# Whole-width loads, a contiguous gMLP, and the V loads on ScalarE's queue in a decode step of attention plus gMLP

## The chip, the cores and the metric

The kernel runs on one core of a Trainium2 chip. The core has five engines with instruction streams of their own: TensorE (PE; its weight loads are listed as PEld), VectorE (DVE), ScalarE (ACT), GpSimd (POOL) and SyncE (SP). Loads and stores are done by 16 DMA engines, to which SP, ACT and POOL hand work through queues; each such engine issues its DMAs in the order of its own instruction stream. The metric is the device time of one execution in microseconds. A profiled execution gives a span (first to last instruction) and a trace.

## What is computed

x is a batch of 4 rows of 640 numbers, normalized to xn. One branch is attention of one query token over a cache of 4096 keys and values, for 32 heads of 128, the other a gMLP block with a hidden size of 864 after the split:

```python
    x = A_x
    xn = _layernorm(x, axis=-1)
    return x + _A_ref(xn, A_k_cache, A_v_cache, A_wq, A_wo) + _B_ref(xn, B_w_in, B_w_sp, B_b_sp, B_w_out)
```

```python
    q = (lambda x, *d: x.transpose(*d))((x @ wq).reshape(B, Sq, H, Dh), 0, 2, 1, 3)
    scores = jnp.einsum('bhqd,bhkd->bhqk', q, k_cache) * Dh ** (-0.5)
    p = _softmax(scores, axis=-1)
    o = jnp.einsum('bhqk,bhkd->bhqd', p, v_cache)
    return (lambda x, *d: x.transpose(*d))(o, 0, 2, 1, 3).reshape(B, Sq, H * Dh) @ wo
```

```python
    z = _gelu(jnp.einsum('bsd,df->bsf', x, w_in))
    z1 = z[..., :Fh].copy()
    z2 = _layernorm(z[..., Fh:], axis=-1)
    g = jnp.einsum('ts,bsf->btf', w_sp, z2) + b_sp[None, :, None]
    return jnp.einsum('bsf,fd->bsd', z1 * g, w_out)
```

The K and V caches are bfloat16 and hold 134 MB each; every byte of them is read once.

## The kernel before

The cache is cut into 32 units of K and 32 of V, called K0 to K31 and V0 to V31 here. A unit is four heads of one batch row, 4096 KB, laid over all 128 partitions, 32 KB in each. Four units in a row (the four batch rows) share their four heads and form one of 8 groups; a softmax is done once for each group.

All big loads share one pool of five buffers, `kvpool`, of one unit each (L66, L85): first the gMLP weights w_in and w_out (L98, L100; w_out on 108 partitions, since 864 = 8 x 108), then the query weights wq in two parts (L107), then K and V units in turn (`load_unit`, L283). A load into a buffer waits until the buffer's last user is done. All of these loads are issued by SP, which has hardly anything else in its stream and so stands waiting at the next free buffer. The output weights wo of a group come into a buffer of their own (`load_wo`, L291). For groups 5 and 6 that load is cut by partitions into 112, 8, 8 and 112, 12, 4 (L464); the last group's comes in three parts by head, ahead of V31 in SP's stream. V31 itself is loaded in four pieces (L475).

A static loop over steps (L476) writes the work down. In a step VectorE transposes a quarter of a K unit (`emit_T`, L305; two buffers for its result), TensorE multiplies the quarter before it with the queries (`emit_S`, L323), and a quarter of a V unit that lies 18 steps behind is multiplied with the probabilities (`emit_V`, L409). At the end of a group come the maximum (L330, L334, L345), the exponentials on ScalarE (L351), their transposes on TensorE (L364), and the copies on ScalarE which place them in `Zb` (L375). After each second V unit ScalarE copies the sums out of PSUM (`emit_O`, L417). The pool for those copies has three buffers and is shared with the probabilities p (tags at L350 and L416). Every four V units the output projection adds to `proj` (L447), an accumulator in PSUM that the kernel opened with x times an identity (L195).

The loop's order is not yet the order on the engines. The framework orders each engine's instructions by its own planner when the program is built, gives the pool's buffers out in that order, and adds the semaphores. What an engine waits for is then fixed: an instruction in an engine's stream stands behind all those before it.

V31 is handled apart: its 128 slices of 128x128 are weights of small matmuls (L520) that follow the pieces as they land; then come the last product with 1/rowsum (L521), the last projection, one copy (L525) and two stores (L526, L527).

At the start, x comes over ScalarE's queue (L92), the two scalars w_sp and b_sp of the gMLP over GpSimd's (L203, L204). VectorE copies the scalars (L215, L216), does the layer norm (L123 to L136), and TensorE does the gMLP's first product in 80 matmuls (L212), whose weights are read from w_in at a stride of 8 elements.

Of the kernel before, what the change touches and what calls it, by code (L numbers as in the profile page):

```python
# [8 lines left out]
ACT = mybir.ActivationFunctionType  # L9
ALU = mybir.AluOpType  # L10
AX = mybir.AxisListType
F32 = mybir.dt.float32
BF16 = mybir.dt.bfloat16
# [3 lines left out]
def kernel(  # L17
# [19 lines left out]
    nc = tc.nc  # L37
    P = 128
    B, Sq, D = A_x.shape
    _, H, Sk, Dh = A_k_cache.shape  # L40
    assert Sq == 1 and B == 4 and Dh == P and D % P == 0
    DC = D // P
    HG = 4
    M = P // HG
    T = Sk // M
    NCH = 4
# [3 lines left out]
    NG = H // HG  # L50
    NU = NG * B
    G = HG * B
    F2 = B_w_in.shape[1]
    Fh = F2 // 2
    FC = next(c for c in range(1, Fh + 1) if Fh % c == 0 and Fh // c <= P)
    FP = Fh // FC
    NOUT = A_wo.shape[1]
    NH = 2
    NO2 = NOUT // NH
    scale = float(Dh) ** -0.5  # L60
    eps = 1e-5
    VD = B * NCH + 2

    const = ctx.enter_context(tc.tile_pool(name="const", bufs=1))
# [4 lines left out]
    wopool = ctx.enter_context(tc.tile_pool(name="wopool", bufs=1))  # L69
# [4 lines left out]
    ps_g = ctx.enter_context(tc.tile_pool(name="ps_g", bufs=1, space=bass.MemoryType.PSUM))  # L74
# [4 lines left out]
    def misc_ps(shape, dtype):  # L79
        misc_ctr[0] += 1  # L80
        return ps_m.tile(shape, dtype, tag="misc", name=f"misc{misc_ctr[0]}")

    KV = T * Dh

    def kv_tile(name):  # L85
        return kvpool.tile([P, KV], BF16, tag="kv", name=name)


    x_flat = A_x.rearrange("b s d -> (b s) d")
    out_flat = out.rearrange("b s d -> (b s) d")  # L90
    x_bf = const.tile([B, D], BF16)
    nc.scalar.dma_start(out=x_bf[:], in_=x_flat)  # L92


    wg = kv_tile("w_gmlp")
    n_in = DC * F2
    w_in = wg[:, 0:n_in].rearrange("p (c f) -> p c f", c=DC)
    nc.sync.dma_start(out=w_in, in_=B_w_in.rearrange("(p c) f -> p c f", c=DC))  # L98
    w_out = wg[:FP, n_in:n_in + FC * NOUT].rearrange("p (c n) -> p c n", c=FC)
    nc.sync.dma_start(out=w_out, in_=B_w_out.rearrange("(p c) n -> p c n", c=FC))  # L100

    wq_v = A_wq.rearrange("(p c) n -> p c n", c=DC)
    wq_t = []
    for i, (c0, c1) in enumerate(((0, 3), (3, DC))):
        wt = kv_tile(f"wq{i}")
        n = (c1 - c0) * H * Dh
        nc.sync.dma_start(out=wt[:, 0:n].rearrange("p (c n) -> p c n", c=c1 - c0), in_=wq_v[:, c0:c1, :])  # L107
        for c in range(c0, c1):
            wq_t.append(wt[:, (c - c0) * H * Dh:(c - c0 + 1) * H * Dh])


    ident_bf = const.tile([P, P], BF16)
# [3 lines left out]
    ones_f = const.tile([P, P], F32)  # L116
    nc.vector.memset(ones_f[:], 1.0)
    eps_t = const.tile([P, 1], F32)
# [1 line left out]

    lnb = wt[:B, KV // 2:KV // 2 + 6 * D].bitcast(F32)
    xf, xc, sq = lnb[:, 0:D], lnb[:, D:2 * D], lnb[:, 2 * D:3 * D]
    nc.vector.tensor_copy(out=xf, in_=x_bf[:])  # L123
    ssum = small.tile([B, 1], F32, tag="ln_s")
    nc.vector.reduce_sum(out=ssum[:], in_=xf, axis=AX.X)
    negmean = small.tile([B, 1], F32, tag="ln_m")
# [38 lines left out]
    for bb in range(2):  # L165
        nc.vector.tensor_copy(out=SelG[:, bb, :, :, 2 * bb:2 * bb + 2],
                              in_=I32[:].rearrange("p (b h c) -> p c h b", b=2, c=NCH))
# [13 lines left out]
    for hd in range(HG):  # L181
        nc.vector.tensor_copy(out=Pm[:, :, hd, :].rearrange("p (a w) j -> p a w j", w=2),
                              in_=ident_bf[:].rearrange("p (a j w) -> p a w j", a=2, w=2))
# [7 lines left out]


    proj = ps_j.tile([64, 512], F32)
    for hf in range(NH):
        nc.tensor.matmul(proj[32 * hf:32 * hf + 32, 0:NO2], lhsT=ident_bf[:B, 0:32],  # L195
                         rhs=x_bf[:, hf * NO2:(hf + 1) * NO2], start=True, stop=False)


    wsp_bf = const.tile([P, 1], BF16)
    bsp_bf = const.tile([P, 1], BF16)  # L200
    wsp_f = const.tile([P, 1], F32)
    bsp_f = const.tile([P, 1], F32)
    nc.gpsimd.dma_start(out=wsp_bf[:], in_=B_w_sp.rearrange("a b -> (a b)").to_broadcast((P, 1)))  # L203
    nc.gpsimd.dma_start(out=bsp_bf[:], in_=B_b_sp.to_broadcast((P, 1)))  # L204

    zT_ps = ps_g.tile([FP, 2, FC, B], F32)

    for fc in range(FC):
        for part in range(2):
            w = w_in[:, :, part * Fh:(part + 1) * Fh].rearrange("p c (f a) -> p c a f", a=FC)  # L210
            for c in range(DC):
                nc.tensor.matmul(zT_ps[:, part, fc, :], lhsT=w[:, c, fc, :],  # L212
                                 rhs=xnT[:, c, :], start=(c == 0), stop=(c == DC - 1))

    nc.vector.tensor_copy(out=wsp_f[:], in_=wsp_bf[:])  # L215
    nc.vector.tensor_copy(out=bsp_f[:], in_=bsp_bf[:])  # L216
    zT = const.tile([FP, 2, FC, B], F32)
    nc.scalar.activation(out=zT[:], in_=zT_ps[:], func=ACT.Gelu_apprx_tanh)  # L218
    z1 = zT[:, 0, :, :]
    z2 = zT[:, 1, :, :]  # L220
    st_in = const.tile([FP, 2, FC, B], F32)
    nc.vector.tensor_copy(out=st_in[:, 0], in_=z2)  # L222
    nc.vector.tensor_tensor(out=st_in[:, 1], in0=z2, in1=z2, op=ALU.mult)
    st_ps = misc_ps([FP, 2, FC, B], F32)
    nc.tensor.matmul(st_ps[:].rearrange("p s c b -> p (s c b)"), lhsT=ones_f[:FP, :FP],
                     rhs=st_in[:].rearrange("p s c b -> p (s c b)"), start=True, stop=True)
    st = const.tile([FP, 2, B], F32)
    nc.vector.tensor_reduce(out=st[:], in_=st_ps[:].rearrange("p s c b -> p s b c"), axis=AX.X, op=ALU.add)
    mean = const.tile([FP, B], F32)
    nc.vector.tensor_scalar(out=mean[:], in0=st[:, 0, :], scalar1=1.0 / Fh, scalar2=None, op0=ALU.mult)  # L230
    msq = const.tile([FP, B], F32)
    nc.vector.tensor_tensor(out=msq[:], in0=mean[:], in1=mean[:], op=ALU.mult)
    var = const.tile([FP, B], F32)
    nc.vector.scalar_tensor_tensor(out=var[:], in0=st[:, 1, :], scalar=1.0 / Fh, in1=msq[:],
                                   op0=ALU.mult, op1=ALU.subtract)
    rs = const.tile([FP, B], F32)
    nc.scalar.activation(out=rs[:], in_=var[:], func=ACT.Sqrt, bias=eps_t[:FP, 0:1], scale=1.0)
    nc.vector.reciprocal(out=rs[:], in_=rs[:])
# [12 lines left out]
    for h in range(H):
        for c in range(DC):
            nc.tensor.matmul(q_ps[:, h, :], lhsT=wq_t[c][:, h * Dh:(h + 1) * Dh], rhs=xnT[:, c, :],  # L253
                             start=(c == 0), stop=(c == DC - 1))
# [3 lines left out]
    for kw in range(4):  # L258
        nc.tensor.matmul(q3_ps[:, kw, :], lhsT=Pm[:, kw, :, :].rearrange("p a j -> p (a j)"), rhs=q_bf[:],
                         start=True, stop=True)  # L260
    q3 = const.tile([P, 4, H * B], BF16)
    nc.vector.tensor_copy(out=q3[:], in_=q3_ps[:])

    for fc in range(FC):
        for hf in range(NH):
            nc.tensor.matmul(proj[32 * hf:32 * hf + B, 0:NO2], lhsT=uT[:, fc, :],
                             rhs=w_out[:, fc, hf * NO2:(hf + 1) * NO2], start=False, stop=False)

    def fill_qz(g):
        qz = QZ[g % 2]  # L270
# [9 lines left out]
    wo_q = A_wo.rearrange("(g p c) n -> g p c n", p=P, c=HG)  # L280
    state = {}

    def load_unit(cache, key, u, cuts=(0, T)):  # L283
        g, b = divmod(u, B)
        t_sb = kv_tile(f"{key}{u}")
        src = cache[b, g * HG:(g + 1) * HG].rearrange("e (m t) d -> (e m) (t d)", t=T)
        for t0, t1 in zip(cuts[:-1], cuts[1:]):
            nc.sync.dma_start(out=t_sb[:, t0 * Dh:t1 * Dh], in_=src[:, t0 * Dh:t1 * Dh])
        state[(key, u)] = t_sb

    def load_wo(g, cuts=(0, P)):  # L291
        wo_t = wopool.tile([P, HG, NOUT], BF16, tag="wo", name=f"wo{g}")
        if g < NG - 1:
            for p0, p1 in zip(cuts[:-1], cuts[1:]):
                nc.sync.dma_start(out=wo_t[p0:p1], in_=wo_q[g, p0:p1])
        else:
            for h0, h1 in ((0, 2), (2, 3), (3, 4)):
                nc.sync.dma_start(out=wo_t[:, h0:h1, :], in_=wo_v[:, g * HG + h0:g * HG + h1, :])
        state[("wo", g)] = wo_t

    def emit_T(u, ch):
        kw = state[("k", u)][:].bitcast(F32)
# [158 lines left out]
        nc.vector.tensor_tensor(out=state["oL"][:, :, b0:b0 + nb], in0=oh[:, :, 0:nb],  # L461
                                in1=state[("rinv", g)][:, :, b0:b0 + nb], op=ALU.mult)

    WO_CUTS = {NG - 3: (0, 112, 120, 128), NG - 2: (0, 112, 124, 128)}  # L464
    sched = {}

    def at(s, fn):
        sched.setdefault(s, []).append(fn)

    for g in range(NG):  # L470
        at(max(0, NCH * B * g - 3), lambda g=g: fill_qz(g))
        at(min(NCH * B * g + VD + 11, NCH * (NU - 1) + VD), lambda g=g: load_wo(g, WO_CUTS.get(g, (0, P))))

    NS = NCH * NU + VD
    TAIL = (0, 64, 96, 112, 128)  # L475
    for s in range(NS):  # L476
        u, ch = divmod(s, NCH)
        if ch == 0 and u < NU:
            load_unit(A_k_cache, "k", u)
        v, vc = divmod(s - VD, NCH)  # L480
# [7 lines left out]
        if 0 <= us < NU:  # L488
            emit_S(us, cs_)
            if us % B == B - 1 and cs_ == NCH - 1:  # L490
                g = us // B
# [4 lines left out]
        if 0 <= v < NU - 1:  # L496
            emit_V(v, vc)
            g, b = divmod(v, B)
# [8 lines left out]
        elif v == NU - 1 and vc == 0:  # L507

            g = NG - 1
# [48 lines left out]
```

## Time and profile before

| | |
|---|---|
| median of 13 runs | 684.55 us (681.93 to 685.48) |
| the profiled execution, device time | 682.63 us |
| its span | 680.6 us |
| TensorE busy | 344.6 us (51%) |
| VectorE busy | 318.9 us (47%) |
| ScalarE busy | 60.3 us (9%) |
| read from HBM | 282.24 MB, 415 GB/s over the span |
| K units, issue to landing, median | 47.0 us |
| V units, issue to landing, median | 41.1 us |
| transposes L305 | 128 of 2278 ns, 284.2 us |
| score matmuls L323 | 1024, 200.7 us |
| V matmuls L409 | 992, 88.5 us |

The span runs from the first to the last instruction; the device time is longer by what lies around it. "Idle before, releaser" behind a group of instructions names what ended most of the engine's idle time. A window line gives, for a stretch of time, its length, the busy time of the five engines with the number of their instructions, the granted TensorE clock, the mean busy share of the 16 DMA engines, and their rate in GB/s. A wait line names the engine and line that waited, for whom, the sum in us, how often, and the longest.

### The profile page before, as it was taken

What the parts mean: (1) busy time and instruction counts of PE and PEld (TensorE: products, weight loads), DVE (VectorE), ACT (ScalarE), POOL (GpSimd) and SP (SyncE); (2) the same over time, 40 slices, a digit from 0 to 9 for tenths busy, and PEclk for the clock granted to TensorE, in tenths of its full rate; (3) what the DMA queues carried; (4) which work ended last, traced back from release to release, by engine and by line L of the source; (5) the groups of instructions that cost most, each with busy time, mean ns of one, the idle gap of its engine ahead of it and who ended that gap; (6) DMA issues with size and microseconds to landing.
All of it is one profiled execution on the core that took longest, in us unless ns stands there. A gap on an engine that the chain in (4) does not pass through costs nothing.

```text
span 680.6 us, 6424 instructions
## 1 busy us (share of the span) xinstructions
PE 344.6 (51%) x2793; PEld 152.0 (22%) x2793; DVE 318.9 (47%) x251; ACT 60.3 (9%) x183; POOL 10.1 (1%) x42
## 2 busy tenths in 40 slices
PE   0967553557434744426445464337644175442655
PEld 0941121123111311103111131112211031110423
DVE  4049873465543355553435654334555235554200
ACT  0010040012000300003000120002100030000300
POOL 1010000000000000000000000000000000000000
PEclk9998877767767787567786677786876668666676
DMA  8999999999999999999999999999999999999994
GB/s 263 433 429 430 430 430 433 430 434 428 433 432 428 429 431 430 431 430 430 428 430 428 437 430 431 430 426 432 429 430 433 334 430 430 431 428 335 431 412 195
DMA packets 11916, 282.66 MB, mean 415 GB/s; under 512 B 1400, under 2 KB 1924, under 8 KB 3076
## 3 DMA queue, kind: packets, MB, share of 16 engines
q1 hardware_dynamic: 11808, 282.25, 98.4%
q8 instruction: 22, 0.36, 0.2%
q14 instruction: 6, 0.05, 0.0%
q10 hardware_dynamic: 16, 0.01, 0.0%
q0 software_dynamic: 64, 0.00, 0.0%
HBM read 282.24 MB, written 0.01 MB: 415 GB/s over the span
## 4 chain that ended last, share of the span: by engine, by line
DMA 56%; PE 14%; issue 13%; DVE 13%; ACT 3%; POOL 0%; DVEq 0%; ACTq 0%; POOLq 0%
DMA k<-in_A_k_cache_dram 45%; DMA v<-in_A_v_cache_dram 10%; DVE kT L305 9%; PE O L409 4%; PE S L323 3%; PE zT_ps L212 2%; ACT p L351 2%; DMA bsp_bf<-in_B_b_sp_dram 2%; PE misc L426 1%; PE x L364 1%; DVE m L330 1%; PE misc L253 1%; DVE om L429 1%; PE misc L334 1%; ACT O_sb L417 0%
## 5 line engine op out<-in xcount | busy, mean ns | idle before, releaser
L305 DVE STREAM_TRANSPOSE kT<-k 128x2048 f32<-128x2048 f32 x128 | 284.2, 2278 | 212.9 <-DMA k<-in_A_k_cache_dram 210.7
L323 PE MATMUL S<-kT,QZ 128*32 128x512 bf16 x1024 | 200.7, 531 | 260.9 <-DVE kT L305 258.5
L323 PEld LDWEIGHTS <-QZ 128*32 128x32 bf16 x1024 | 56.7, 114 | 401.3 <-issue 388.3
L409 PE MATMUL O<-v,Zb 128*32 128x512 bf16 x992 | 88.5, 450 | 7.0 <-DMA v<-in_A_v_cache_dram 7.0
L409 PEld LDWEIGHTS <-Zb 128*32 128x32 bf16 x992 | 42.4, 109 | 34.9 <-issue 16.7
L351 ACT ACTIVATE p<-S,negmax 128x1024 bf16<-128x1024 f32 x16 | 17.7, 1110 | 282.2 <-DVE negmax L345 282.2
L417 ACT COPY O_sb<-O 128x512 f32<-128x512 f32 x16 | 9.4, 586 | 234.9 <-PE O L409 234.9
L375 ACT COPY Zb<-x 32x128 bf16<-32x128 bf16 x128 | 27.3, 254 | 10.2 <-PE x L364 9.4
L364 PE MATMUL x<-IdP,p 128*128 128x128 bf16 x128 | 16.1, 305 | 18.9 <-ACT p L351 18.5
L429 DVE SCALAR_TENSOR_TENSOR om<-misc,rinv,MkH 16x512 bf16<-16x512 f32 x7 | 5.2, 738 | 39.5 <-PE misc L426 39.5
L426 PE MATMUL misc<-O_sb,SelG 128*16 128x128 f32 x112 | 18.3, 306 | 3.8 <-ACT O_sb L417 1.5
L364 PEld LDWEIGHTS <-p 128*128 128x128 bf16 x128 | 12.0, 138 | 22.8 <-ACT p L351 22.8
L212 PEld LDWEIGHTS <-w_gmlp 128*108 128x108 bf16 x80 | 16.0, 295 | 0.1
L212 PE MATMUL zT_ps<-xnT,w_gmlp 128*108 128x4 bf16 x80 | 15.9, 336 | 0.3 <-DVE xnT L142 0.3
L274 POOL COPY QZ<-q 32x16 bf16<-32x16 bf16 x32 | 7.9, 246 | 457.5 <-PE S L323 412.3
L426 PEld LDWEIGHTS misc<-O_sb,SelG 128*16 128x16 f32 x112 | 10.5, 104 | 10.1 <-ACT O_sb L417 4.6
L461 DVE TENSOR_TENSOR oL<-misc,rinv 128x8 bf16<-128x8 f32 (+1 forms) x2 | 0.3, 168 | 21.5 <-PE misc L459 21.5
L330 DVE TENSOR_REDUCE m<-S 128x1 f32<-128x512 f32 x8 | 5.5, 692 | 10.1 <-PE S L323 10.1
L355 DVE TENSOR_TENSOR rowsum<-rs 128x1 f32<-128x1 f32 x8 | 1.2, 154 | 17.0 <-ACT p L351 17.0
L334 PE MATMUL misc<-dg,ones_f 128*128 128x128 f32 x16 | 4.3, 356 | 9.0 <-DVE dg L332 9.0
L140 PE MATMUL misc<-ident_bf,wq 4*128 4x4 bf16 x5 | 0.4, 178 | 14.7 <-DVE wq L136 14.7
L222 DVE COPY st_in<-zT 108x32 f32<-108x32 f32 x1 | 0.2, 181 | 16.2 <-ACT zT L218 16.2
(92 smaller groups left out, 81.6 us busy)
## 6 DMA issues: line engine op xcount, KB each, us to landing
k<-in_A_k_cache_dram SPq DMA_DIRECT2D x32, 4096.0 KB, 47.0
v<-in_A_v_cache_dram SPq DMA_DIRECT2D x31, 4096.0 KB, 41.1
wo<-in_A_wo_dram SPq DMA_DIRECT2D x5, 640.0 KB, 45.7
wq<-in_A_wq_dram SPq DMA_DIRECT2D x1, 3072.0 KB, 22.3
w_gmlp<-in_B_w_in_dram SPq DMA_DIRECT2D x1, 2160.0 KB
wq<-in_A_wq_dram SPq DMA_DIRECT2D x1, 2048.0 KB, 26.8
v<-in_A_v_cache_dram SPq DMA_DIRECT2D x1, 2048.0 KB
wo<-in_A_wo_dram SPq DMA_DIRECT2D x2, 560.0 KB, 48.8
```

Source lines behind the costliest of these rows:

```text
L212: nc.tensor.matmul(zT_ps[:, part, fc, :], lhsT=w[:, c, fc, :], rhs=xnT[:, c, :], start=(c == 0), stop=(c == DC - 1))
L305: nc.vector.transpose(kT[:], kw[:, ch * n:(ch + 1) * n])
L323: nc.tensor.matmul(S_ps[32 * q:32 * q + 32, :, :], lhsT=qz[:, b, kw, w0:w0 + 32], rhs=kT[:, i, :, kw // 2, :, kw % 2], start=(b == 0 and c ...
L330: nc.vector.tensor_reduce(out=m1[:], in_=S_ps[:].rearrange("p k m -> p (k m)"), axis=AX.X, op=ALU.max)
L334: nc.tensor.matmul(mm[:], lhsT=ones_f[:], rhs=dg[:], start=True, stop=True)
L351: nc.scalar.activation(out=p_i[:], in_=S_ps[:, 8 * i:8 * i + 8, None, :].to_broadcast((P, 8, HG, M)), func=ACT.Exp, bias=negmax[:, 0:1], s ...
L364: nc.tensor.transpose(x[:, t, :], p_bf[t // 8][:, t % 8].rearrange("p h m -> p (h m)"), IdP[:])
L375: nc.scalar.copy(out=dst, in_=src[:, 2 * bb + b1])
L409: nc.tensor.matmul(O_ps[32 * q:32 * q + 32, :, :], lhsT=Zb[bb][:, w0:w0 + 32], rhs=vv[:, e // 16, e % 16, :, :], start=(b1 == 0 and e < 4) ...
L417: nc.scalar.copy(out=O_sb[:], in_=O_ps[:])
L426: nc.tensor.matmul(oh[:], lhsT=SelG[:, bb, c].rearrange("p h b -> p (h b)"), rhs=O_sb[:, c, :], start=(bb == 0 and c == 0), stop=(bb == 1 ...
L429: nc.vector.scalar_tensor_tensor(out=om[:], in0=oh[:, None, :].to_broadcast((G, HG, Dh)), scalar=state.pop(("rinv", g))[:, 0:1], in1=MkH[: ...
```

## The change

1. w_in and w_out are taken in contiguous chunks of 128 columns or rows: seven chunks, the last of 96. w_out is loaded as 768 rows on 128 partitions and 96 rows on 96. The 80 matmuls become 70, with weights that lie side by side. The statistics run over all 128 partitions, with zeros in the unused part.
2. The scalars and x are issued on ScalarE's queue, x last of the three; x lies in the buffer of wq's second part.
3. x is added to `proj` late, by two matmuls from a small buffer `x_res` that SP loads in the middle of the kernel.
4. The wo loads of groups 5 and 6 are no longer cut. The last group's wo takes a buffer of `kvpool`, and its three loads stand behind V31's four in SP's stream.
5. The loads of V0 to V30 are issued by ScalarE, K, wo and V31 by SP.

```diff
-    FC = next(c for c in range(1, Fh + 1) if Fh % c == 0 and Fh // c <= P)
-    FP = Fh // FC
+    FC = (Fh + P - 1) // P
+    FL = Fh - (FC - 1) * P
...
-    w_out = wg[:FP, n_in:n_in + FC * NOUT].rearrange("p (c n) -> p c n", c=FC)
-    nc.sync.dma_start(out=w_out, in_=B_w_out.rearrange("(p c) n -> p c n", c=FC))
+    w_out = wg[:, n_in:n_in + FC * NOUT].rearrange("p (c n) -> p c n", c=FC)
+    nf = (FC - 1) * P
+    nc.sync.dma_start(out=w_out[:, 0:FC - 1, :], in_=B_w_out[0:nf, :].rearrange("(c p) n -> p c n", p=P))
+    nc.sync.dma_start(out=w_out[:FL, FC - 1, :], in_=B_w_out[nf:Fh, :])
...
+    x_bf = wt[:B, KV // 2 + 7 * D:KV // 2 + 8 * D]
+    nc.scalar.dma_start(out=x_bf, in_=x_flat)
+    sb_bf = const.tile([P, 2], BF16)
+    nc.scalar.dma_start(out=sb_bf[:, 0:1], in_=B_w_sp.rearrange("a b -> (a b)").to_broadcast((P, 1)))
+    nc.scalar.dma_start(out=sb_bf[:, 1:2], in_=B_b_sp.to_broadcast((P, 1)))
...
-    nc.gpsimd.dma_start(out=wsp_bf[:], in_=B_w_sp.rearrange("a b -> (a b)").to_broadcast((P, 1)))
-    nc.gpsimd.dma_start(out=bsp_bf[:], in_=B_b_sp.to_broadcast((P, 1)))
...
-            w = w_in[:, :, part * Fh:(part + 1) * Fh].rearrange("p c (f a) -> p c a f", a=FC)
+    for part in range(2):
+        for fc in range(FC):
+            n = P if fc < FC - 1 else FL
+            f0 = part * Fh + fc * P
             for c in range(DC):
-                nc.tensor.matmul(zT_ps[:, part, fc, :], lhsT=w[:, c, fc, :],
+                nc.tensor.matmul(zT_ps[:n, part, fc, :], lhsT=w_in[:, c, f0:f0 + n],
                                  rhs=xnT[:, c, :], start=(c == 0), stop=(c == DC - 1))
...
+    zT = const.tile([P, 2, FC, B], F32)
+    nc.vector.memset(zT[:], 0.0)
+    uT = const.tile([P, FC, 32], BF16)
+    nc.vector.memset(uT[:], 0.0)
+    nc.scalar.activation(out=zT[:, :, 0:FC - 1, :], in_=zT_ps[:, :, 0:FC - 1, :], func=ACT.Gelu_apprx_tanh)
+    nc.scalar.activation(out=zT[:FL, :, FC - 1, :], in_=zT_ps[:FL, :, FC - 1, :], func=ACT.Gelu_apprx_tanh)
...
+        eng = nc.scalar if key == "v" and u < NU - 1 else nc.sync
         src = cache[b, g * HG:(g + 1) * HG].rearrange("e (m t) d -> (e m) (t d)", t=T)
         for t0, t1 in zip(cuts[:-1], cuts[1:]):
-            nc.sync.dma_start(out=t_sb[:, t0 * Dh:t1 * Dh], in_=src[:, t0 * Dh:t1 * Dh])
+            eng.dma_start(out=t_sb[:, t0 * Dh:t1 * Dh], in_=src[:, t0 * Dh:t1 * Dh])
...
-    def load_wo(g, cuts=(0, P)):
-        wo_t = wopool.tile([P, HG, NOUT], BF16, tag="wo", name=f"wo{g}")
+    def load_wo(g):
         if g < NG - 1:
-            for p0, p1 in zip(cuts[:-1], cuts[1:]):
-                nc.sync.dma_start(out=wo_t[p0:p1], in_=wo_q[g, p0:p1])
+            wo_t = wopool.tile([P, HG, NOUT], BF16, tag="wo", name=f"wo{g}")
+            nc.sync.dma_start(out=wo_t[:], in_=wo_q[g])
         else:
+            wo_t = kv_tile("wo_last")[:, 0:HG * NOUT].rearrange("p (h n) -> p h n", h=HG)
             for h0, h1 in ((0, 2), (2, 3), (3, 4)):
                 nc.sync.dma_start(out=wo_t[:, h0:h1, :], in_=wo_v[:, g * HG + h0:g * HG + h1, :])
...
+    x_res = const.tile([32, NO2], BF16)
+    nc.vector.memset(x_res[:], 0.0)
+    def load_x():
+        nc.sync.dma_start(out=x_res[0:32:4, :], in_=x_flat.rearrange("b (h n) -> (b h) n", h=NH))
+    def add_x():
+        for hf in range(NH):
+            nc.tensor.matmul(proj[32 * hf:32 * hf + B, 0:NO2], lhsT=ident_bf[:32, 4 * hf:32:8], rhs=x_res[:],
+                             start=False, stop=False)
...
-    WO_CUTS = {NG - 3: (0, 112, 120, 128), NG - 2: (0, 112, 124, 128)}
...
-        at(min(NCH * B * g + VD + 11, NCH * (NU - 1) + VD), lambda g=g: load_wo(g, WO_CUTS.get(g, (0, P))))
+        at(NCH * (NU - 1) + VD if g == NG - 1 else NCH * B * g + VD + 11, lambda g=g: load_wo(g))
+    at(NCH * (NU - 2) + VD, load_x)
+    at(NCH * (NU - 1) + VD, add_x)
```

In the built program the V loads stand among ScalarE's other work. The stretch from V15's load to V21's, in ScalarE's order, is: load V15, load V16, exp of K16 to K19, O copy of V14 and V15, load V17, the Zb copies, load V18, O copy of V16 and V17, load V19, exp of K20 to K23, load V20, half of the Zb copies, O copy of V18 and V19, the other half, load V21. At the end it is: exp of K28 to K31, load V28, half of the Zb copies, O copy of V26 and V27, the other half, load V29, load V30, O copy of V28 and V29, O copy of V30. The buffers that these loads wait for were last held by: V16 by K18, V17 by K19, V18 by K20, V19 by V16, V20 by K22, V31 by K31.

## The prediction

> **What bounds the kernel now.** I read the page's slices first, then its DMA part, the waits of the DMA queue, and short windows where the rate of the slices falls. The slices, and the queues below them:
>
> ```profile
> DMA  8999999999999999999999999999999999999994
> GB/s 263 433 429 430 430 430 433 430 434 428 433 432 428 429 431 430 431 430 430 428 430 428 437 430 431 430 426 432 429 430 433 334 430 430 431 428 335 431 412 195
> ...
> q1 hardware_dynamic: 11808, 282.25, 98.4%
> ```
>
> The DMA engines are the bound: they stand at 430 GB/s in all but five slices (of 17 us), and one queue, SyncE's, carries everything. 282.66 MB at 430 GB/s are 657.3 us of the 680.6. So only the remaining 23 us can be won, and anything that leaves the engines without work is lost at once. A K or V unit (4096 KB, 4.19 MB) takes 9.75 us. The windows cut the five weak slices finer (columns after the busy times: TensorE clock, DMA share, GB/s):
>
> ```profile
> 0.00:6.00 6.00, 0.44 (x2) 0.19 (x2) 4.72 (x24) 1.28 (x1) 2.24 (x10) 1.00 0.74 254
> 6.00:16.00 10.00, 0.00 (x0) 0.00 (x0) 2.79 (x8) 0.00 (x0) 0.00 (x0) 1.00 0.93 261
> 530.00:542.00 12.00, 0.00 (x0) 0.00 (x0) 2.10 (x1) 0.00 (x0) 0.00 (x0) 0.57 1.00 291
> 542.00:552.00 10.00, 7.22 (x34) 2.05 (x33) 8.21 (x8) 0.00 (x0) 0.00 (x0) 0.66 1.00 427
> 612.00:624.00 12.00, 0.00 (x0) 0.00 (x0) 1.22 (x1) 0.00 (x0) 0.00 (x0) 0.71 1.00 289
> 656.00:670.00 14.00, 7.37 (x64) 3.40 (x56) 0.34 (x2) 1.17 (x2) 0.00 (x0) 0.69 0.97 395
> 670.00:676.00 6.00, 3.75 (x124) 3.50 (x125) 0.00 (x0) 0.00 (x0) 0.00 (x0) 0.63 0.31 126
> ```
>
> Loss of a window = length x (1 - rate/430): 2.5 us for 0-6, 3.9 for 6-16, 3.9 for 530-542, 3.9 for 612-624, 1.1 and 4.2 for 656-676. In the three middle dips the DMA share is 0.93 to 1.00: the engines are busy, but slow. They lie where w_out on 108 partitions (issued at 1.17) and the wo loads cut into 112+8+8 and 112+12+4 partitions (issued at 493.1 and 575.5, landing some 45 us later) pass. The five uncut wo loads leave no dip. Compute is not the bound; who waits for whom:
>
> ```profile
> DVE kT L305 <- DMA k<-in_A_k_cache_dram: 210.7, 21, 15.1
> PE S L323 <- DVE kT L305: 258.5, 125, 14.6
> ACT O_sb L417 <- PE O L409: 234.9, 16, 30.8
> ```
>
> VectorE waits for K, TensorE for VectorE, ScalarE for TensorE. A unit of K needs 8.9 us of transposes (four of 2.22) and a V unit 2 to 3.6 us of matmuls, of 19.5 us that a pair's loads take. The end, from the timeline:
>
> ```profile
> 664.05 3.60 PE L409 MATMUL O<-v,Zb 128*32 128x512 bf16 x32 [4.60 <-DMA v<-in_A_v_cache_dram]
> 667.71 0.59 ACT L417 COPY O_sb<-O 128x512 f32<-128x512 f32 x1 [9.37 <-PE O L409]
> 668.35 1.06 PE L459 MATMUL misc<-I,O_sb 128*128 128x8 f32 x8 [0.69 <-ACT O_sb L417]
> 675.66 0.59 PE L520 MATMUL ol<-Zb,v 128*128 128x4 bf16 x16 [0.66 <-DMA v<-in_A_v_cache_dram]
> 678.29 0.29 SPq L526 DMA_DIRECT2D out_dram<-o_bf  x1
> ```
>
> The last piece of V31 (32 units, 0 to 31) lands at 675.6; only 16 small matmuls, the projection, one copy and the store follow: 5.0 us.
>
> **What the Trainium skill says.** "DMA: Bandwidth & Descriptors", section on issuing engines not being separate DMA queues: loads from ScalarE and SyncE run on the same 16 engines and interleave; a second issuer saves issue time alone. The trace agrees as far as it goes: 98.4% of engine time is one queue's and it already reaches 430. Its section on queues and rings says that an engine alternates between rings packet by packet, so I give two busy rings half the rate each; no run here shows it yet. Its section on why a DMA adds 16 says that the number of engines is the largest up to 16 that divides the partitions (108: 12; 96: 16; 8: 8), and "SBUF — State Buffer", section on the DMA port swizzle, that partitions map to ports in a fixed way; loads of odd partition counts thus leave the even engine-to-port match. The three dips agree.
>
> **Part by part.** *Whole loads.* Both wo dips go: -3.9 -3.9. w_out becomes 768 rows on 128 partitions and 96 rows on 96: of its 3.9 I keep 1.3 for rows of 1280 bytes and the odd 96, so -2.6 (bounds 0 and -3.9). Uneven engines at the end (5.3 us in 656-676) come in part from those dips; I take 2.3 left, -3 (bounds 0 and -5). Sum -13.4.
>
> *gMLP, scalars, x.* Weight loads at a stride cost 295 ns (L212, 80 of them, 15.9 us); the contiguous ones of the query (L253, 157 in 4.34 us) pass at 28 ns each, so 70 take 2 us: -14 us on TensorE. The two waits of VectorE for the scalars (4.5 and 2.6 us) shrink, since ScalarE's queue issues them at once; x now stands behind them, a microsecond or two. All of this only readies the queries before K0 has landed (issued at 3.5, landing 34.2 later: 37.7 us) instead of at 46.5. DMA ran at 415 from 16 us on while compute lagged, so it is worth 0; nothing else becomes late, the next K buffers merely come free sooner. Uncovered it would be worth up to 14. The memsets, the second gelu call, the 5 KB load and two matmuls of x_res lie under loads: 0.
>
> *V on ScalarE's queue.* SyncE does nothing else, so it waited at a free buffer and issued early. ScalarE runs in order: behind a waiting load stand exp, the Zb copies and the O copies, and a load stands behind them. The order of the built instructions shows for units 16 to 23: V17 stands behind exp(K16-19) and the O copy of V14,15; that copy takes a buffer that the probabilities hold until the transposes which TensorE runs after K20's scores. So V17 is issued 8.9 (transposes) + 1.1 (scores) + 2.1 (transposes of p) + 0.6 (copy) = 12.7 us after K20 lands. V20 stands behind exp(K20-23): 8.9 + 1.1 + 2.65 (max to exp, from 226.63 and 229.30) + 2.2 (two exps) = 14.9 us after K23 lands. V19 waits for the copy of V16,17, V21 for that of V18,19.
>
> Does a ring run dry? By hand, with pairs of 19.5 us: K20's landing at 0 finds on SyncE's ring K21 (half gone, 5 us left) and K22 (its buffer came free with V15's matmuls; 9.75), and V16 on ScalarE's. V16 is over at about 14, when V17's data starts. At K23's landing the SyncE ring holds K24, two thirds left, and K25, free since V18 was used: some 16 us of work, against 14.9 + 1 of start. If ScalarE's ring is empty for some microseconds, K takes the whole rate: no loss. Cost in the middle 0, with V19's rest on top some 9 us of margin; bounds 0 and 3 us a softmax.
>
> At the end this cover is gone. After K31 no K is left; V31 (SyncE) waits for K31's own buffer, so 8.9 + about 1.2 to its first byte, and V28 stands behind exp(K28-31), 14.9. Before, V28 to V30 were issued between 589.8 and 612.4, ahead of K31's use at 622.8. Now only V27's rest covers. V27 is issued after the copy of V24,25; K31 and V26 end some 3 us apart, so V27 has run 3 us at half rate and 8.2 are left, less a microsecond between last byte and signal: loss 3 (bounds 0.4 and 10).
>
> Then V31, V28, V29, V30 pass, and V30 is last instead of the short last piece of V31. What stands behind its landing: 3.6 (32 matmuls) + 0.1 + 0.59 (copy) + 1.1 (L459) + all 128 small matmuls of V31, at 28 ns, 3.6 + 0.3 + 1.2 (projection) + 0.5 (copy) + 2.3 (store and end) + 0.1 = 13.4, against 5.0: +8.4. wo_last's last piece waits on V29's signal, 9.7 us earlier: 0.
>
> Sum: -13.4 + 3 + 8.4 = -2.0 on the span, 678.6. The profiled execution has 682.63 with 680.6 of span, so 680.6; the median of 13 runs lies 1.9 above it, so about 682.5 as a median, -0.3%. 0.2% (1.4 us) is about what a measurement can tell from no change.
>
> **Rivals.** *The rings run dry at each softmax (slower).* Place: from the landing of a group's last K to the next V load. It decides once SyncE's ring holds under 15 us of work there, that is, once the K two further is issued later than 5 us after that landing. For it: V19 and K25 depend on buffers freed by V units that are now late. Against: about one load of margin by the count above. 1.5 us in each of 7 softmaxes: +10.5, 693. *V27 is over before K31:* the gap is 10 instead of 3: +7, 689.5. For: V27's issue hangs on an O copy; against: the stagger above. *Shared rings do not halve evenly or V31 comes last after all:* V28 to V30 pass first, the tail stays 5, 674. For: nothing in the trace forbids it; against: V30's late issue. *The dips stay, or two rings cost a percent of rate:* +8, 690.5. For: two rings were never seen together; against: wo0 to wo4 run whole without a dip.
>
> **How the numbers follow.** Forecast 50% (679 to 686: 33 faster, 12 same, 5 slower), dry rings 20%, gap of 10 us 12%, short tail 12%, dips or rate 6%. Faster 0.45, same 0.12, slower 0.43. For eight in ten the range reaches 672 to 694; the forecast's own is 679 to 686.
>
> **What would show it.** Right: no slice near 334 in the middle, a dip after K31's landing (near 610), V30 landing last, 13 us from there to the end, 128 L536 matmuls in one row. Wrong: slices under 420 at each softmax (dry rings), a steady rate under 425 (two rings), V31's last piece landing after V30, or VectorE idle for K in blocks longer than 15 us.

## The result, and the profile after

The kernel after takes 690.28 us (median of 11 runs, 689.33 to 691.71), the kernel before 684.34 in the runs beside it. The ratio is 1.0091, 95% interval 1.0079 to 1.0103: 0.9% slower. The profiled execution has a span of 688.5 us against 680.6, so 7.9 us have to be explained. (The medians are 5.9 us apart: the profiled execution of before was 1.7 us faster than the median of its runs.)

The slices of the page and the queues below them, after:

```profile
GB/s 319 429 434 428 431 430 428 434 428 434 426 430 431 430 430 431 432 429 435 431 430 427 426 432 436 425 432 433 431 426 436 425 431 430 429 422 126 439 438 46
...
q1 hardware_dynamic: 8104, 152.23, 52.0%
q10 hardware_dynamic: 4768, 130.03, 44.0%
```

Two things that the prediction asked for are there: the slices of 334 and 335 in the middle are gone, and two queues (q10 is ScalarE's) share the load at an unchanged 430 GB/s. One thing is far larger than forecast: a slice of 126, where K31 lands. Windows of 6 us around it (after the busy times: TensorE clock, DMA share, GB/s):

```profile
612.00:618.00 6.00, 0.00 (x0) 0.00 (x0) 0.00 (x0) 0.00 (x0) 0.00 (x0) 0.50 0.99 426
618.00:624.00 6.00, 0.00 (x0) 0.00 (x0) 1.40 (x1) 0.00 (x0) 0.00 (x0) 0.50 0.42 180
624.00:630.00 6.00, 4.62 (x31) 1.62 (x32) 6.00 (x4) 0.00 (x0) 0.00 (x0) 0.61 0.00 0
630.00:636.00 6.00, 1.99 (x14) 0.63 (x9) 3.10 (x6) 0.93 (x1) 0.00 (x0) 0.96 0.62 218
```

By the prediction's own rule, length x (1 - rate/430), the loss is 3.5 + 6.0 + 3.0 = 12.5 us, where the prediction had 3. The timeline shows why nothing was under way:

```profile
598.68 0.33 ACTq L291 DMA_DIRECT2D v<-in_A_v_cache_dram  x1
...
622.60 8.89 DVE L320 STREAM_TRANSPOSE kT<-k 128x2048 f32<-128x2048 f32 x4 [19.94 <-DMA k<-in_A_k_cache_dram]
631.52 1.85 SPq L291 DMA_DIRECT2D v<-in_A_v_cache_dram  x4
635.18 0.33 ACTq L291 DMA_DIRECT2D v<-in_A_v_cache_dram  x1
...
674.54 3.60 PE L424 MATMUL O<-v,Zb 128*32 128x512 bf16 x32 [6.01 <-DMA v<-in_A_v_cache_dram]
678.20 0.59 ACT L432 COPY O_sb<-O 128x512 f32<-128x512 f32 x1 [10.78 <-PE O L424]
...
680.56 3.55 PE L536 MATMUL ol<-Zb,v 128*128 128x4 bf16 x128
...
686.16 0.29 SPq L542 DMA_DIRECT2D out_dram<-o_bf  x1
```

The first line is the issue of V27. K31 lands at 622.5, and by the windows everything issued is over at 624. The next issues are V31's four pieces at 631.52, when K31's buffer is free, and V28 at 635.18, behind the exp. The last lines are the tail: V30's landing at 674.5 releases its 32 matmuls, and 14.0 us lie from there to the end of the span (forecast 13.4, before 5.0), with all 128 matmuls of V31 in one row behind it.

So of the 7.9 us, the gap is +12.5 and the longer tail +9.0, less what the other parts gained. What remains is why V27 had nothing left when K31 landed. V27 was issued right behind its O copy, as assumed. But V26 and K31 were to end some 3 us apart, so that V27 would have run beside K31 for 3 us. In the trace V26 is first waited for and used here:

```profile
607.13 2.75 PE L424 MATMUL O<-v,Zb 128*32 128x512 bf16 x24 [3.31 <-DMA v<-in_A_v_cache_dram]
```

That is 15.5 us before K31 (622.60), and in this time V27 passed. The DMA view of the stretch in which wo6 passes, 584.3 to 601.2 us, after (packets, MB, share of 16 engines' time):

```profile
q10 hardware_dynamic: 186, 5.57, 76.7%
q1 hardware_dynamic: 180, 1.63, 22.8%
```

The two queues moved nearly the same number of packets, 186 and 180, but 5.57 MB against 1.63. A wo load is 128 packets of 5 KB on SyncE's queue; a V packet has 32 KB. That gave the theory tested below: two rings take turns by the packet, not by bytes or time, so wo6 held K31 back while V26 and V27 passed. By bytes, SyncE's queue would have had half of the 7.2 MB, so K 3.6 less wo6's 0.66, 2.9 MB; it had 0.97. The 2 MB are 4.6 us of the whole rate, taken from K and given to V. The load before it, wo5, shows the same; from 509.2 to 520.7 us:

```profile
q10 hardware_dynamic: 139, 4.06, 82.5%
q1 hardware_dynamic: 146, 0.81, 17.1%
```

### The profile page after: what moved, and what is told of

Its sections match the earlier page's. It is cut to its first block, busy times and chain, and to the rows that moved or that the text cites. A ratio compares the mean times of both kernels' runs of the same rounds, so it can differ in the third digit from the quotient of the medians.

```text
span 688.5 us, 6412 instructions
## 1 busy us (share of the span) xinstructions
PE 312.4 (45%) x2781; PEld 127.8 (19%) x2781; DVE 319.5 (46%) x253; ACT 59.9 (9%) x184; POOL 9.0 (1%) x40
## 4 chain that ended last, share of the span: by engine, by line
DMA 73%; PE 9%; DVE 9%; issue 7%; ACT 1%; ACTq 0%; DVEq 0%
DMA k<-in_A_k_cache_dram 52%; DMA v<-in_A_v_cache_dram 20%; DVE kT L320 6%; PE O L424 4%; PE S L338 2%; DMA sb_bf<-in_B_b_sp_dram 1%; PE x L379 1%; PE misc L251 1%; PE ol L536 0%; PE zT_ps L209 0%; DVE m L345 0%; PE proj L267 0%; ACT Zb L390 0%; PE misc L474 0%; DVE om L444 0%
## 5 line engine op out<-in xcount | busy, mean ns | idle before, releaser
L338 PE MATMUL S<-kT,QZ 128*32 128x512 bf16 x1024 | 184.4, 497 | 226.0 <-DVE kT L320 213.8
L424 PE MATMUL O<-v,Zb 128*32 128x512 bf16 x992 | 116.7, 548 | 104.3 <-DMA v<-in_A_v_cache_dram 104.3
L424 PEld LDWEIGHTS <-Zb 128*32 128x32 bf16 x992 | 38.1, 121 | 160.2 <-issue 117.0
L379 PE MATMUL x<-IdP,p 128*128 128x128 bf16 x128 | 11.7, 254 | 6.3 <-ACT p L366 6.3
L441 PE MATMUL misc<-O_sb,SelG 128*16 128x128 f32 x112 | 13.8, 273 | 1.1 <-DVE rinv L400 0.7
L379 PEld LDWEIGHTS <-p 128*128 128x128 bf16 x128 | 9.1, 114 | 12.4 <-ACT p L366 6.9
L462 PE MATMUL proj<-wo,oT 128*4 128x320 bf16 x56 | 7.8, 395 | 0.3 <-DVE oT L455 0.3
L251 PE MATMUL misc<-xnT,wq 128*128 128x4 bf16 x160 | 4.7, 166 | 1.7 <-issue 1.4
```

What stands on the lines that cost most here:

```text
L338: nc.tensor.matmul(S_ps[32 * q:32 * q + 32, :, :], lhsT=qz[:, b, kw, w0:w0 + 32], rhs=kT[:, i, :, kw // 2, :, kw % 2], start=(b == 0 and c ...
L379: nc.tensor.transpose(x[:, t, :], p_bf[t // 8][:, t % 8].rearrange("p h m -> p (h m)"), IdP[:])
L424: nc.tensor.matmul(O_ps[32 * q:32 * q + 32, :, :], lhsT=Zb[bb][:, w0:w0 + 32], rhs=vv[:, e // 16, e % 16, :, :], start=(b1 == 0 and e < 4) ...
L441: nc.tensor.matmul(oh[:], lhsT=SelG[:, bb, c].rearrange("p h b -> p (h b)"), rhs=O_sb[:, c, :], start=(bb == 0 and c == 0), stop=(bb == 1 ...
L462: nc.tensor.matmul(proj[32 * hf:32 * hf + B, 0:NO2], lhsT=oT[:, c, :], rhs=wo_t[:, c, hf * NO2:(hf + 1) * NO2], start=False, stop=(last an ...
```

## The experiments

All times are medians; a ratio is to the kernel before, measured beside it. The edits of e1 to e7 and e9 to e11 are to the kernel after, those of e8 and e12 to the kernel before.

**e1: every V load on SyncE's queue.**

```diff
-        eng = nc.scalar if key == "v" and u < NU - 1 else nc.sync
+        eng = nc.sync
```

> The kernel after with every V load back on SyncE's queue; all other parts of the change stay. Theory (the time goes lost at the end alone: an empty ring after K31's landing, 12.5 us, and the longer tail, 9 us; the other parts save 10 to 17): 666 to 672 us, some 19 to 24 us under the kernel after and about 2% under the kernel before; no dip at 334 or 335 in the slices, V31's last small piece lands last and 5 us follow it. Rival (the other parts save little, and the loads on ScalarE's queue are nearly neutral): 682 to 690 us.

Measured: 670.38 us, ratio 0.9803 (0.9782 to 0.9824). The other parts of the change are worth 13.5 us (684.17 x 0.0197), and the move of V costs about 20. The slices, e1:

```profile
GB/s 311 440 419 436 432 433 421 433 435 426 434 433 425 435 431 429 430 432 430 427 431 431 428 432 428 436 426 431 436 429 428 435 423 433 427 439 425 430 427 245
```

No slice but the first and last falls under 419. This version is 2% faster than the kernel before.

**e2: V28 to V31 on SyncE's queue, V0 to V27 on ScalarE's.**

```diff
-        eng = nc.scalar if key == "v" and u < NU - 1 else nc.sync
+        eng = nc.scalar if key == "v" and u < NU - 4 else nc.sync
```

> The kernel after with V28 to V31 on SyncE's queue, V0 to V27 left on ScalarE's. Theory (two rings cost nothing in the middle): within 2 us of the run with every V on SyncE's queue, 666 to 672 us. Rival (two rings cost something at each softmax or in rate): at least 5 us slower than that run, 673 us or more, with slices below 425 in the middle or a gap at K31 that stays.

Measured: 670.2 us, ratio 0.98 (0.9782 to 0.9818), no different from e1. With 28 of 32 V units on ScalarE's queue nothing is lost, so the whole cost goes when the last three units move, and two rings cost nothing in the middle, the wo loads' packets included. That a K which wo delays there is made up from the buffers is my reading; no run tries it by itself.

**e3: V30 alone on SyncE's queue.**

```diff
-        eng = nc.scalar if key == "v" and u < NU - 1 else nc.sync
+        eng = nc.scalar if key == "v" and u < NU - 2 else nc.sync
```

> The kernel after with V30 alone moved to SyncE's queue, in front of V31 there; V28 and V29 stay behind the exp on ScalarE's. Theory: V30 fills the time after K31's landing in which nothing was under way, so the gap of 12.5 us falls to 4 or less; V29 then lands last in V30's place with a tail of 13 to 15 us: 679 to 683 us, 8 to 11 under the kernel after. Rival (the gap is not one of the rings but of the engines): unchanged, 690 us. Rival 2 (V30 waits for a buffer too): a gap of 8 us or more stays, 687 us.

Measured: 690.87 us, ratio 1.0083 (1.0054 to 1.0113); its runs scatter from 686.39 to 691.45. No gain: rival 2 holds. The waits of SyncE's queue from 590 to 650 us in e3 (us in total, times, longest):

```profile
SPq L291 <- DMA v<-in_A_v_cache_dram: 22.6, 1, 22.6
SPq L291 <- PE S L338: 21.4, 1, 21.4
```

In e3's timeline V30 is issued at 628.20, 5.2 us after K31's first transpose begins (623.04). Its buffer is V26's, and V26's last 8 matmuls stand behind K31's first scores on TensorE. The trace is of the fastest of the five runs: its windows from 618 to 636 us lose 9.2 us, 3.3 less than the gap after, and its span is 3.9 us shorter. How the gap looks in the slower four isn't known. A spare unit in front of the queue is no use if its buffer depends on the same landing.

**e4: wo6 on ScalarE's queue.**

```diff
-            nc.sync.dma_start(out=wo_t[:], in_=wo_q[g])
+            (nc.scalar if g == NG - 2 else nc.sync).dma_start(out=wo_t[:], in_=wo_q[g])
```

> The kernel after with the load of wo6, 128 packets of 5 KB, moved from SyncE's ring to ScalarE's, where it passes between V units. Theory (rings take turns by packet, so that beside 32 KB packets the 128 small packets held SyncE's ring, and with it K30 and K31, for 17 us): K31 lands before V27 is well under way, 5 to 9 us earlier than 622.5, the gap after K31 shrinks from 12.5 us to 2 to 6, and the time falls by 6 to 10 us to 680 to 684. Rival (rings share by bytes, K31 and V27 end together for another reason, V27's late issue behind the O copy): K31 lands within 2 us of before and the time stays within 2 us of 690.

Measured: 680.04 us, ratio 0.9944 (0.9926 to 0.9963): 10 us less than the kernel after, for a load of 0.66 MB. In e4's timeline K31 is used from 611.30 on, and V31's issue follows 10.7 us later:

```profile
611.30 4.50 DVE L320 STREAM_TRANSPOSE kT<-k 128x2048 f32<-128x2048 f32 x2 [6.46 <-DMA k<-in_A_k_cache_dram]
...
621.97 2.91 SPq L291 DMA_DIRECT2D v<-in_A_v_cache_dram  x4
```

K31 comes 11.3 us earlier (5 to 9 were expected), and the page's slice of 126 becomes 354. But wo6 now also holds back V27, which stands behind it; e6 takes that away.

**e5: V28 alone on SyncE's queue**.

```diff
-        eng = nc.scalar if key == "v" and u < NU - 1 else nc.sync
+        eng = nc.scalar if key == "v" and u < NU - 1 and u != NU - 4 else nc.sync
```

> The kernel after with V28 alone moved to SyncE's queue, between K31 and V31; V29 and V30 stay on ScalarE's. Theory (e3 kept its gap since the buffer of V30 is that of V26, whose last 8 matmuls stand behind K31's scores on TensorE; V28 takes the buffer of V25, which is free early): V28 is issued near 600 us, some 20 us before K31 lands, passes in the gap, and 12.5 us of loss become 2 to 4; the tail behind V30 stays 13 to 14 us. 679 to 682 us, 8 to 11 under the kernel after. Rival (every V that is late costs, wherever it stands): 686 to 690 us.

Measured: 680.44 us, ratio 0.9948 (0.993 to 0.9967). V28 was issued at 598.43 and filled the gap. Windows of e5:

```profile
624.00:630.00 6.00, 2.99 (x20) 1.12 (x22) 5.35 (x3) 0.00 (x0) 0.00 (x0) 0.50 0.91 393
630.00:636.00 6.00, 3.75 (x24) 1.16 (x19) 4.52 (x4) 0.00 (x0) 0.00 (x0) 0.83 0.41 126
```

The loss is 0.5 + 4.2 = 4.7 us, a little over the 2 to 4 expected: a unit is 9.75 us, and V31 follows K31 by more.

**e6: wo6 held back until K31 is in use.**

```diff
+            if g == NG - 2:
+                nc.gpsimd.tensor_copy(out=wo_t[0:1, 0, 0:2], in_=state[("kT", NU - 1, 0)][0:1, 0:1].bitcast(BF16))
             nc.sync.dma_start(out=wo_t[:], in_=wo_q[g])
```

> The kernel after with wo6 held back on SyncE's queue until K31's first transpose is done (a copy of 2 values by GpSimd from that transpose into the wo tile, which the load then writes over), so that it stands behind K31; V27's place on ScalarE's queue is not touched. Theory (wo6's 128 packets of 5 KB take 128 turns from K31 and let V26 and V27 pass): K31 lands 7 to 9 us earlier than 622.5, V27 has 6 to 8 us left then, the loss after K31 falls from 12.5 to about 3 as the prediction had it: 679 to 683 us. Rival (rings share by bytes: 0.66 MB moved behind K31 are worth 1.5 us): K31 lands 1 to 2 us earlier, 688 to 690 us.

Measured: 680.61 us, ratio 0.9952 (0.9934 to 0.997). The timeline of e6:

```profile
599.82 0.33 ACTq L291 DMA_DIRECT2D v<-in_A_v_cache_dram  x1
...
611.76 4.50 DVE L322 STREAM_TRANSPOSE kT<-k 128x2048 f32<-128x2048 f32 x2 [8.10 <-DMA k<-in_A_k_cache_dram]
...
614.33 0.33 SPq L299 DMA_DIRECT2D wo<-in_A_wo_dram  x1
...
621.57 2.70 SPq L291 DMA_DIRECT2D v<-in_A_v_cache_dram  x4
```

and its windows:

```profile
612.00:618.00 6.00, 4.66 (x48) 1.95 (x49) 5.23 (x3) 0.00 (x0) 0.17 (x1) 0.65 0.97 411
618.00:624.00 6.00, 2.35 (x18) 0.94 (x17) 4.52 (x4) 0.00 (x0) 0.00 (x0) 1.00 0.73 266
```

V27 is issued at the same point as in the kernel after (599.82 against 598.68). With wo6 out of K31's way, K31 comes 10.8 us earlier (7 to 9 were expected), 1.2 us before V26 instead of 15.5 behind it:

```profile
612.98 2.75 PE L426 MATMUL O<-v,Zb 128*32 128x512 bf16 x24 [8.20 <-DMA v<-in_A_v_cache_dram]
```

The loss is 0.3 + 2.3 = 2.6 us, the prediction's 3. By bytes, 0.66 MB are 1.5 us. The rival falls. The stretch from 584.3 to 601.2 us, in which wo6 passed in the kernel after, now has 32 KB packets on both sides, and each queue gets half:

```profile
q10 hardware_dynamic: 128, 3.67, 50.4%
q1 hardware_dynamic: 123, 3.64, 50.0%
```

**e7: V31's pieces behind V30 on ScalarE's queue.**

```diff
-        eng = nc.scalar if key == "v" and u < NU - 1 else nc.sync
+        eng = nc.scalar if key == "v" else nc.sync
```

> The kernel after with V31's four pieces on ScalarE's queue too, behind V30, so that the short piece lands last again. Theory: the tail behind the last landing falls from 14.0 to 5 us, -9; but the first load after K31 is now V28, issued behind the exp at 635.2 instead of 631.5, so the gap grows by 3.7: net -5, 684 to 687 us. Rival (the longer tail is not what costs, since V31's matmuls could run earlier): 690 to 694 us.

Measured: 686.87 us, ratio 1.0051 (1.0034 to 1.0067), at the upper edge of what was expected. The end of e7:

```profile
680.43 0.59 PE L536 MATMUL ol<-Zb,v 128*128 128x4 bf16 x16 [0.72 <-DMA v<-in_A_v_cache_dram]
...
683.06 0.30 SPq L542 DMA_DIRECT2D out_dram<-o_bf  x1
```

From the last landing to the end of the span (685.4) it is 5.0 us again, 9 less than after. The windows from 618 to 642 us lose 16.3 us in e7, 3.8 more than the gap after, since nothing is issued before V28 at 635.68. So the two costs move apart as expected. The span falls by 3.1, some 2 less than the sum of the two. Of these 2, 1.5 lie just before the last landing, where the engines are no longer all busy (share 0.93; the windows stand under "Why the prediction was wrong").

**e8: the kernel before with whole wo loads.**

```diff
-    WO_CUTS = {NG - 3: (0, 112, 120, 128), NG - 2: (0, 112, 124, 128)}
+    WO_CUTS = {}
```

> The kernel before with wo5 and wo6 loaded whole, over 128 partitions, nothing else. Theory (the loads over 112, 12, 8 and 4 partitions slow all 16 engines for some 12 us each, 3.9 us lost per dip): both dips near 334 go, 7 to 9 us faster, 675 to 678 us. Rival (the dips lie elsewhere in time or the engines catch up later): within 2 us of 684.

Measured: 675.7 us, ratio 0.9887 (0.987 to 0.9904), 7.7 us by the ratio (684.0 x 0.0113). Slices of e8:

```profile
GB/s 253 437 424 427 433 434 431 424 433 431 434 434 423 430 433 433 430 427 433 431 432 434 423 429 436 435 423 433 429 433 436 419 434 429 434 433 424 431 419 183
```

Both dips are gone, and nothing else is needed for over half of the gain of e1.

**e9: V0 to V27 and V31 on SyncE's queue, V28 to V30 on ScalarE's.**

```diff
-        eng = nc.scalar if key == "v" and u < NU - 1 else nc.sync
+        eng = nc.scalar if key == "v" and NU - 4 <= u < NU - 1 else nc.sync
```

> The kernel after with V0 to V27 and V31 back on SyncE's queue and V28 to V30 alone on ScalarE's. Theory (the gap after K31 is that V27 has nothing left then; in one ring V27 stands whole behind K31 and wo6, some 11 us of work): no gap, 430 GB/s through K31's landing; the tail behind V30 stays 13 to 14 us against 5. So 670.4 of the run with every V on SyncE's queue plus 8 to 10: 678 to 681 us. Rival (a late V28 to V30 costs more than the tail, as V31 can't fill the time alone): a gap stays, 684 us or more.

Measured: 679.91 us, ratio 0.9929 (0.9903 to 0.9955). V30's landing in e9:

```profile
664.62 3.24 PE L424 MATMUL O<-v,Zb 128*32 128x512 bf16 x32 [5.70 <-DMA v<-in_A_v_cache_dram]
```

From there to the end of the span (677.3) it is 12.7 us, 7.7 more than e1's tail, and that is most of the 9.5 us above e1. The theory's "no gap" did not come true: 377 and 273 GB/s in the windows from 624 to 636 us lose 2.9 us, about what the prediction had for V27's rest. The stretch just before the last landing gives back 1.4.

**e10: e1 with the 70 matmuls of zT done six times.**

```diff
-    for part in range(2):
+    for part in [0, 1] * 6:
```

> The kernel after with every V load on SyncE's queue (e1), and the 70 matmuls of zT done six times over, the same sums each time: 350 more of 36 ns, some 13 us more on TensorE ahead of the queries, about what the strided weight loads cost. Theory (the compute ahead of K0 is hidden): within 1 us of e1, 670 to 671.5 us. Rival (the early queries bring time, since K0's buffer comes free sooner): 673 to 684 us.

Measured: 671.89 us, ratio 0.9815 (0.979 to 0.984); the single runs, 671.66 to 672.87, lie above those of e1, 670.18 to 670.61, though the intervals overlap. K0's transposes begin at 45.48 us in the timeline, in e1 at 36.94. Windows of e10:

```profile
36.00:46.00 10.00, 8.26 (x213) 7.09 (x214) 3.19 (x14) 1.85 (x4) 0.32 (x2) 1.00 0.98 390
46.00:56.00 10.00, 8.08 (x40) 2.13 (x35) 10.00 (x5) 0.00 (x0) 1.66 (x7) 1.00 0.96 408
```

In e1 these are 428 and 424. The difference is 0.9 + 0.4 = 1.3 us. The answer lies between theory and rival: early queries are worth something, 1 to 1.5 us, less than the rival's range (673 us and more) would need.

**e11: e1 with w_out's load cut into 108 and 20 partitions.**

```diff
-    nc.sync.dma_start(out=w_out[:, 0:FC - 1, :], in_=B_w_out[0:nf, :].rearrange("(c p) n -> p c n", p=P))
+    w_out_d = B_w_out[0:nf, :].rearrange("(c p) n -> p c n", p=P)
+    for p0, p1 in ((0, 108), (108, P)):
+        nc.sync.dma_start(out=w_out[p0:p1, 0:FC - 1, :], in_=w_out_d[p0:p1])
```

> The kernel after with every V load on SyncE's queue (e1), and the load of w_out's 6 whole chunks cut into 108 and 20 partitions. Theory (loads over other numbers of partitions than 128 slow the engines at the start as they did with wo): the window from 6 to 16 us falls from 332 GB/s to 260 to 300, and the time grows by 1.5 to 4 us, to 672 to 674.5. Rival (the start gained from the missing load of x or the scalars): within 0.7 us of e1.

Measured: 674.43 us, ratio 0.9848 (0.9819 to 0.9877). A window of e11:

```profile
6.00:16.00 10.00, 0.00 (x0) 0.00 (x0) 0.00 (x0) 0.00 (x0) 0.00 (x0) 1.00 1.00 248
```

With w_out cut, the start is as slow as before the change (261), with the engines 100% busy; in e1 the same window has 332. The windows up to 26 us lose 2.7 us more than e1's; the spans differ by 4.0 (672.4 and 668.4), and 1.0 of the other 1.3 lies between 645 us and the last landing (363 GB/s; why is open). The cut is 108 and 20 partitions; the kernel before had 108 alone.

**e12: the kernel before with V0 to V30 on ScalarE's queue.**

```diff
+        eng = nc.scalar if key == "v" and u < NU - 1 else nc.sync
         for t0, t1 in zip(cuts[:-1], cuts[1:]):
-            nc.sync.dma_start(out=t_sb[:, t0 * Dh:t1 * Dh], in_=src[:, t0 * Dh:t1 * Dh])
+            eng.dma_start(out=t_sb[:, t0 * Dh:t1 * Dh], in_=src[:, t0 * Dh:t1 * Dh])
```

> The kernel before with the loads of V0 to V30 on ScalarE's queue, nothing else of the change. Theory (that part costs some 20 us by itself, 12 at the gap and 8 to 9 in the tail, whatever the others do): 701 to 707 us, 2.5 to 3.3% slower than before, with a gap near K31's landing and V30's landing some 13 us ahead of the end. Rival (the parts aren't additive, since with two rings the loads over few partitions stand beside V's and their dips are filled): 692 to 698 us.

Measured: 685.99 us, ratio 1.0029 (1.002 to 1.0038), outside both ranges: 2 us instead of 20. The timeline of e12:

```profile
592.24 0.33 SPq L289 DMA_DIRECT2D k<-in_A_k_cache_dram  x1
592.68 1.15 SPq L296 DMA_DIRECT2D wo<-in_A_wo_dram  x3
...
605.19 0.82 ACTq L289 DMA_DIRECT2D v<-in_A_v_cache_dram  x2
...
620.51 4.50 DVE L306 STREAM_TRANSPOSE kT<-k 128x2048 f32<-128x2048 f32 x2 [9.70 <-DMA k<-in_A_k_cache_dram]
```

The same edit makes another order here. K31 (592.24) is issued ahead of wo6 (592.68), and on ScalarE V28 follows V27 at once (605.19, two loads), ahead of the exp. Both supports that the kernel after lacks are there, so there is no gap; the dips of the cut wo loads stay (323 GB/s in the windows from 618 to 630 us), and V30's landing at 670.3 leaves 13.2 us of tail, 8.2 more than before. That these 8.2 cost only 2 has two reasons in the trace. Up to V30's landing the queues are full: the stretch from 645 us loses 0.9 us, where the kernel before loses 5.1 before its last landing. And loads still pass behind V30's landing, 146 GB/s or 2.0 us of the whole rate:

```profile
670.30:676.30 6.00, 5.27 (x70) 2.78 (x71) 0.17 (x1) 0.59 (x1) 0.00 (x0) 0.70 0.37 146
```

So 8.2 - 4.2 - 2.0 = 2.0 (the spans differ by 2.9). Which of the two supports would do alone was not tried in this kernel. The run shows that the cost of moving the loads is not fixed: it depends on what the program's order puts ahead of the last K and the exp.

## Why the prediction was wrong

Forecast 0.3% faster, measured 0.9% slower. Its parts, against what the runs showed:

- **Whole loads, -13.4: right in size, one part by luck.** e1 has 13.5 in all, with 1 to 1.5 of gMLP in it. The two wo dips, -7.8, are e8's 7.7. For w_out -2.6 was taken, and e11's start shows 2.7. The uneven engines at the end, -3, were to come in part from those dips. Here is the stretch from 645 us to the last landing (in e12 and e9 V30's), in the order before, e8, e1, e7, e12, e9, after:

```profile
645.00:675.70 30.70, 17.95 (x245) 10.15 (x246) 1.25 (x4) 2.88 (x10) 0.00 (x0) 0.71 0.86 359
645.00:668.40 23.40, 14.42 (x192) 9.13 (x191) 0.34 (x2) 1.17 (x2) 0.00 (x0) 0.50 0.83 342
645.00:663.40 18.40, 12.08 (x186) 7.81 (x178) 0.34 (x2) 1.17 (x2) 0.00 (x0) 0.59 0.90 372
645.00:680.40 35.40, 17.82 (x239) 9.96 (x238) 1.25 (x4) 1.72 (x5) 0.00 (x0) 0.66 0.93 391
645.00:670.30 25.30, 8.87 (x84) 3.81 (x84) 0.34 (x2) 0.59 (x1) 0.00 (x0) 0.67 0.99 415
645.00:664.60 19.60, 7.13 (x78) 3.51 (x78) 0.64 (x3) 0.61 (x2) 0.00 (x0) 0.72 0.97 407
645.00:674.50 29.50, 8.79 (x86) 3.92 (x86) 0.87 (x3) 0.64 (x2) 0.00 (x0) 0.69 0.96 406
```

  By the same rule they lose 5.1, 4.8, 2.5, 3.2, 0.9, 1.1 and 1.7 us. e8 took both dips away and its end is as uneven as before, so the dips were not the reason. In the first four the small pieces of V31 land last, in the last three the stretch ends with a whole V30. The kernel after gains 3.4 us here, close to the 3, for another reason than the one given: luck. The prediction also explained the dips by partition counts that leave the even match of engines and ports. e8 and e11 show that the cut loads make the dips; no run tries the reason. In the dips the engines are busy and slow (share 0.93 to 1.00), and why is open.
- **gMLP, scalars, x, worth 0: nearly.** The 70 matmuls take 2.5 us (2 forecast) where the 80 took 15.9. The prediction put that down to the stride and set 295 ns, the mean length of one strided weight load, beside 28 ns, the time from one contiguous matmul to the next; by the second measure the 80 took 198 ns each. Nor is the stride shown to be all of it: after, contiguous loads of 96 columns last 187 ns on average, those of 128 columns 105, and the strided ones had 108 columns. The queries are ready 10 us earlier, as predicted (K0's transposes begin at 36.46 instead of 46.47), and e10 puts some 1 to 1.5 us on that. The waits for the scalars did not shrink: VectorE waits 7.0 us in one piece where it waited 4.5 and 2.6, and ScalarE's queue brought the two-byte values no sooner. That cost nothing, as it was hidden.
- **The middle, 0: right.** e2 and e1 are equal. "Dry rings" was no case.
- **The tail, +8.4: right as a length.** 9.0 by the trace (14.0 - 5.0); e7 takes it back and e9 has 7.7 of it with a small gap. What it costs is less where the stretch ahead of it runs fuller, as e7, e9 and e12 show.
- **The end gap, loss 3 (bounds 0.4 and 10): this step failed.** It measured 12.5. The argument was that V27, issued after the copy of V24 and V25, has run 3 us at half rate when K31 lands, so that 8.2 us are left. The issue was as said; "half rate", and with it the 3 us between the ends of V26 and K31, was not: they were 15.5 us apart. The prediction quoted the Trainium skill, "DMA: Bandwidth & Descriptors", section "Queues, rings and completion order", for engines that take turns between rings packet by packet, and then gave each ring half of the rate. This follows only for equal packets. The trace agrees with the page's sentence (186 packets against 180), and with wo6's 5 KB packets on one side and V's of 32 KB on the other it meant 23% of the engines' time against 77%, where e6 has 50% against 50%. wo6 in front of K31 was not counted at all; by its bytes it is 1.5 us, beside V it took 17. The prediction had cost the wo loads under "whole loads" alone, and their place ahead of K31 under the second ring nowhere. e6 restores the premise and gets 2.6 us.

With 12.5 in place of 3 and 9.0 in place of 8.4, the prediction's own sum is -13.4 + 12.5 + 9.0 = +8.1; the span grew by 7.9. So close an agreement is partly chance: e1's gain is 13.5 by the medians but 12.2 between the profiled spans (680.6 and 668.4), so the sum holds to 1 or 2 us. The rival "V27 is over before K31", given 12% and 689.5 us, named the right place and nearly the right size, but for another reason (a late issue of V27 behind its O copy, which did not happen). That its 689.5 lies near the measured 690.28 is luck.

## What to carry to other kernels

Before a stream of loads is split over two queues, look at the packet size on each side: a small transfer with short packets costs its own queue one long packet of the other queue per turn, and whatever stands behind it comes late by that. In the middle of the stream that cost nothing here, at the end it cost some 10 us (e4, e6), so the last units should stand on a queue that issues them as soon as a buffer is free, and not behind an engine's own arithmetic. Check the order of the built program rather than the edit: the same line cost 20 us in one kernel and 2 in the other.

## What the runs showed that was not expected

- Two rings share by packets almost evenly: 186 to 180 packets in 16.9 us, 5.57 to 1.63 MB. A load of 640 KB in 5 KB packets, some 1.5 us at 430 GB/s, took 11.5 us (wo5) and 17 us (wo6) beside 32 KB packets. An estimate from these runs gives the first: 128 packets are eight for each of the 16 engines, a 32 KB packet takes 1.22 us (a unit's 9.75 us x 16 / 128), a 5 KB one 0.19, and eight turns of both are 11.3 us. In wo6's stretch some 30 packets of K passed too (0.97 MB).
- Two busy rings together reach the same 430 GB/s as one, no more and no less (slices of e1 and after). This agrees with the Trainium skill, "DMA: Bandwidth & Descriptors", section "Issuing engines are not separate DMA queues", by which both issuers' loads run on the same 16 engines and a second one saves issue time alone; the kernel before, with its one queue, could not show it.
- A load over 108 or 112 partitions goes with a stretch of 10 to 12 us in which the 16 engines are busy (share 0.93 to 1.00) and move 248 to 291 GB/s: e8 takes it away, and e11 brings it back.
